# Value product in bursts over eight query blocks instead of four, with V fetched per head group from DRAM

## The chip, the cores and the metric

The kernel runs on one core of one Trainium2 chip. The metric is device time in microseconds (us), from the runs of the program before the change: 726.66, 725.91 and 726.65 us, median 726.65 us. One further execution was taken with the hardware profiler; it lasted 726.8 us.

## What is computed

Two branches of one block are mixed by a learned gate. Branch A is attention over 2048 positions with 32 heads of 16 columns and a sliding causal window of 256; branch B is a gated linear unit.

```python
qkv = x @ wqkv                                    # x: 2048 x 512
scores = einsum("bhqd,bhkd->bhqk", q, k) * 16 ** -0.5
mask = (i - j >= 0) & (i - j < 256)               # i: query, j: key
p = softmax(where(mask, scores, -1e9))
a = einsum("bhqk,bhkd->bhqd", p, v) @ wo
b = (sigmoid(x_ @ w_gate) * (x_ @ w_up)) @ w_down # x_ is the same x
g = sigmoid((x * gate_w).sum(-1))
return g * a + (1 - g) * b
```

All of it is fp32. The kernel takes one x for both branches.

## The kernel before

**Tiles and stages.** The 2048 positions are 16 blocks of 128. The 32 heads are 8 head groups of 4. So attention has 128 steps, called blocks here and `u` in the code; `u // 16` is the head group. The first 40 us project V and the first queries and keys. Then the loop over `u` runs from 0 to 137 (lines 796 to 919), and the last stage (lines 969 to 1032) multiplies by `w_down` and `wo` and writes the output.

**What a block does.** For each of the 4 heads, called a slot here, TensorE computes the scores of query block `u` (`s_part`, line 334, tile `s`). VectorE adds the mask and takes each row's maximum (line 350, tile `junk`); this is called the reduction below. Nine blocks later TensorE computes the transposed scores of key block `u - 9` (`st_part`, line 385, tile `st`), with the maxima already inside through an extra row of the operands, and ScalarE takes the exponential into the tile `pbuf` (line 397). When all four heads of a block are there, GpSimd clears what lies outside the window with one or two `affine_select` (`mask_p`, lines 403 and 409). `s` and `st` have two PSUM banks each: the scores of a slot wait for the reduction of two slots before, the transposed scores for the exponential of two slots before.

**Side work on TensorE.** The `s` and `st` matmuls use half of the array's rows (64). In the other time both halves work through the gate and up projections (`gu`), the projections of later head groups (`pj`) and a tail (`tp`). One step of this is a turn: one 64x512 matmul on each half. `GAPS` (line 44) says how many turns follow each slot: twelve times 3, three times 2; the sixteenth slot of four blocks has none. Each such group is accumulated over 24 matmuls in one of three `misc` banks; a ScalarE copy (line 523 or 269) empties it before the group three further on may start.

**The value product.** Every four blocks, from `u = 13` on, there is a visit: `pv_part` (line 418) multiplies a strip of four query blocks by V. The four heads stand side by side in columns of 32 (`tile_position`), all 128 rows are used, in plain fp32:

```python
for j in range(j0, q0 + 4):
    q, e = max(j, q0), min(j + 3, q0 + 4)
    for hh in range(HG):
        v = j * VROW + (g * HG + hh) * VW
        mm(pv[32 * hh:32 * hh + 32, ...], Vf[:, v:v + 32], p_blk(...), ...)
```

It is written into the one bank `pv` and copied out by ScalarE (`o_take`, line 435) into the tile `ob`. Its last column of ones gives the softmax sums.

**The maxima.** At the same visits `max_split` (line 357) takes the sixteen maxima of a strip through three small VectorE instructions (lines 360, 361, 365), `max_store` sends them to DRAM and `max_load` brings them back as rows of the operand ring. The strip is the one whose transposed scores begin two blocks later.

**What sets the order.** The order on TensorE, ScalarE, VectorE and the SP queue, which issues the DMAs, is written out by this loop. Side work of VectorE (low parts of split operands, list `behind`) is taken at slots 1, 5 and 9 after a visit, that of ScalarE (list `acts`) at any slot but the last three. V lies in SBUF for all heads (tile `V`, block after block); `pbuf` holds 15 block places.

Of the kernel before, what the change touches and what calls it, by code (L numbers as in the profile page):

```python
# [14 lines left out]
P = 128  # L15
# [3 lines left out]
H = 32  # L19
# [13 lines left out]
VROW = H * VW  # L33
SCALE = DH ** -0.5
# [5 lines left out]
PVLAG = LAG + 4  # L40
SD = 3
QB = 32
HOLD = 3
GAPS = [3] * 12 + [2] * 3
SHIFT = 6
# [9 lines left out]
AHEAD = 7  # L55
H_LOAD = {126: (0,), 130: (1, 2), 134: (3, 4), 137: (5, 6)}
# [3 lines left out]
def gated_mix_kernel(  # L60
# [37 lines left out]
    stack_d = nc.dram_tensor("stack_scratch", (RING, 2, P, CH2), F32, kind="Internal").ap()  # L98
    fill_d = nc.dram_tensor("fill_scratch", (2, CH2), F32, kind="Internal").ap()
# [39 lines left out]
    with ExitStack() as actx:  # L139
# [4 lines left out]

        Vf = apool.tile([P, NB * VROW + 16], F32, name="V")
        Vh = Vf[:, 0:NB * VROW].rearrange("p (b h w) -> p b h w", b=NB, w=VW)
# [22 lines left out]
        xraw = Vf[:, NB * VROW + 16 - 2 * ND * CH:].rearrange("p (c d t) -> p c d t", c=2, d=ND)  # L169
# [57 lines left out]
        def fill_v(b0, b1):  # L227
            if b1 == NB:
                nc.gpsimd.memset(Vf[:, NB * VROW:], 0.0)
            nc.gpsimd.memset(Vh[:, b0:b1, :, DH:VW], 1.0)  # L230

        fill_v(0, NB // 2)

# [5 lines left out]
        def v_part(b, d):  # L239
# [4 lines left out]
            if d == ND - 1:  # L244
                nc.scalar.copy(Vh[:, b, :, 0:DH], vp.pop(b).rearrange("p (h w) -> p h w", w=DH))
# [21 lines left out]
        def proj_raw(s):  # L267
            raws[s] = cpool.tile([P, CH], F32, tag="sp", name=f"pr{s}", bufs=4)
            nc.scalar.copy(raws[s], pj[s])
            pj[s] = raws.pop(s)  # L270
# [86 lines left out]
        def max_split(s):  # L357
# [6 lines left out]
            nms[s] = spool.tile([P, QB], F32, tag="nt", name=f"nt{s}")  # L364
# [15 lines left out]

        def p_blk(u, hh, a, n):
            s0, step = homes[u // 4 % 2][u % 4]
            return pbuf[:, s0 + a * step:s0 + (a + n - 1) * step + 1:step, hh]
# [17 lines left out]
        def mask_p(u):  # L401
            s0, step = homes[u // 4 % 2][u % 4]
            nc.gpsimd.affine_select(  # L403
                pbuf[:, s0], pbuf[:, s0], pattern=[[0, HG], [1, P]], compare_op=ALU.is_ge,
                fill=0.0, base=0, channel_multiplier=-1,
            )
            if u % NB + 2 < NB:
                old = pbuf[:, s0 + 2 * step]
# [9 lines left out]
        def pv_part(s):  # L418
# [3 lines left out]
            for j in range(j0, q0 + 4):  # L422
                q, e = max(j, q0), min(j + 3, q0 + 4)
                for hh in range(HG):
                    v = j * VROW + (g * HG + hh) * VW
                    mm(  # L426
                        pv[32 * hh:32 * hh + 32, (q - q0) * P:(e - q0) * P],
                        Vf[:, v:v + 32],
# [4 lines left out]
            evac.append(lambda: o_take(s))  # L433

        def o_take(s):
            g, c = divmod(s, NC)
            ob = cpool.tile([P, CH], F32, tag="ob", name=f"ob{s}", bufs=1)
            nc.scalar.copy(ob, pv)
# [28 lines left out]
        def v_out(b):  # L467
            nc.scalar.copy(Vh[:, b, :, 0:DH], vq[b].rearrange("p (h w) -> p h w", w=DH))
# [52 lines left out]
        def gu_post(f, c, w):  # L521
            t = cpool.tile([P, CH], F32, tag="sp", name=f"sp{f}_{c}_{w}", bufs=4)
# [42 lines left out]
        def tail_post(b):  # L565
            t = cpool.tile([P, CH], F32, tag="sp", name=f"tt{b}", bufs=4)
# [34 lines left out]
        def v_sum(b):  # L601
            lower, upper = halves.pop(f"vh{b}")
            t = cpool.tile([P, CH], F32, tag="sp", name=f"vsum{b}", bufs=4)
            nc.scalar.copy(t, lower)
            heads = lambda v: v.rearrange("p (h w) -> p h w", w=DH)
            behind.append(lambda: nc.vector.tensor_tensor(Vh[:, b, :, 0:DH], heads(upper), heads(t), op=ALU.add))
# [8 lines left out]
        def proj_sum(s):  # L615
            lower, upper = halves.pop(f"ph{s}")
            t = cpool.tile([P, CH], F32, tag="sp", name=f"psum{s}", bufs=4)
# [37 lines left out]
        def turns():  # L655
# [3 lines left out]
            sizes = GAPS * ((NU - PVLAG + 4) // 4) + GAPS[0:12]  # L659
            sizes += [6] * 14  # L660
            for size in sizes:
                for _ in range(size):
# [4 lines left out]
                    for half, v in enumerate((t, t - SHIFT)):  # L667
                        if 0 <= v < n_rest * k3:
# [3 lines left out]
                            if k == 0 and n in ended and size > 3:  # L672
# [118 lines left out]

        proj_at = {5: [5], LAG: [6, 7], U_LAST: [NSTEP - 2], U_LAST + 1: [NSTEP - 1]}
# [291 lines left out]
```

## Time and profile before

| what | value |
|---|---|
| median of the runs | 726.65 us |
| profiled execution, and the span of its trace | 726.8 us, 725.1 us |
| TensorE busy in the span (matmul, weight load) | 719.6 us, 590.4 us |
| VectorE, ScalarE, GpSimd busy | 485.0, 422.4, 163.5 us |
| value product matmuls (line 426) | 1408 records, 32 visits, from 83.1 to 553.3 us |
| reductions (line 350) | 512, mean 0.53 us |
| clock granted to TensorE | full speed in every slice |

A matmul's row gives its start and a modelled end, and matmuls overlap, so TensorE reads as busy nearly all the time whether or not its array is filled. What a piece costs is therefore read from the distance between the starts of the matmuls around it. An fp32 matmul leaves two records (passes): a visit of 24 matmuls has 48.

### The profile page before, as it was taken

Reading aid. Unit: us, or ns where it says so; the run is one execution under the profiler, and the core shown is the slowest. Engines: PE = TensorE matmul, PEld = TensorE weight load, DVE = VectorE, ACT = ScalarE, POOL = GpSimd, SP = SyncE. Lnnn points to the kernel's source line nnn. Section 1 sums busy time; section 2 is a strip of 40 time slices with the busy share of each in tenths; the row PEclk is TensorE's granted clock in tenths of the full one; section 3 lists DMA queues with packets and bytes.
Section 4 is the critical chain, followed back from the end, with each engine's and each line's share of the span. In section 5 each row is a group of like instructions: output and inputs, shape, how many; then the busy total and the mean of one; then the engine's idle time right before and its main releaser. Section 6 shows DMA issues by size and latency. Waiting matters only on the chain.

```text
span 725.1 us, 17392 instructions
## 1 busy us (share of the span) xinstructions
PE 719.6 (99%) x6298; PEld 590.4 (81%) x6298; DVE 485.0 (67%) x1455; ACT 422.4 (58%) x890; POOL 163.5 (23%) x255
## 2 busy tenths in 40 slices
PE   9999999999999999999999999999999999999997
PEld 7888888888888788887888877888788888888886
DVE  5368767666775676767677676677837777667481
ACT  6423766666576576756667666665666654535341
POOL 5200333232233223323223332322431000000000
PEclk9999999999999999999999999999999999999999
DMA  8442335444454543454444355354478897878431
GB/s 291 123 117 80 126 128 209 158 151 132 148 189 151 190 132 132 157 184 166 154 148 162 116 197 184 131 187 141 132 226 209 220 256 192 227 173 245 141 67 58
DMA packets 99502, 118.30 MB, mean 163 GB/s; under 512 B 46526, under 2 KB 59326, under 8 KB 99416
## 3 DMA queue, kind: packets, MB, share of 16 engines
q1 hardware_dynamic: 99272, 117.07, 52.2%
q8 instruction: 49, 0.80, 0.5%
q14 instruction: 37, 0.30, 0.1%
q10 hardware_dynamic: 144, 0.13, 0.1%
HBM read 67.34 MB, written 46.67 MB: 157 GB/s over the span
## 4 chain that ended last, share of the span: by engine, by line
PE 98%; DMA 1%; SPq 0%; issue 0%; ACT 0%; DVE 0%; DVEq 0%
PE gu L257 28%; PE pj L257 12%; PE pv L426 11%; PE s L344 7%; PE st L392 6%; PE tp L561 6%; PE pd L89 5%; PE pd L88 5%; PE pd L90 5%; PE vh L598 3%; PE pa L88 2%; PE pa L90 2%; PE pa L89 2%; PE vps L464 1%; DMA V<-in_xT_dram 1%; PE pd L1011 1%
## 5 line engine op out<-in xcount | busy, mean ns | idle before, releaser
L350 DVE CUSTOM_DVE_ANT_0 junk<-s,mask 128x384 f32<-128x384 f32 (+2 forms) x512 | 272.1, 531 | 138.8 <-PE s L344 69.8
L397 ACT ACTIVATE pbuf<-st 128x384 f32<-128x384 f32 (+2 forms) x512 | 240.9, 477 | 161.9 <-PE st L392 105.9
L257 PE MATMUL gu<-xh,w 64*128 64x512 f32 x1152 | 271.0, 393 | 0.0
L257 PE MATMUL gu<-xl,w 64*128 64x512 f32 x576 | 182.5, 391 | 0.0
L403 POOL TENSOR_SCALAR_AFFINE_SELECT pbuf<-pbuf 128x512 f32<-128x512 f32 x128 | 82.7, 646 | 368.7 <-ACT pbuf L397 368.7
L392 PE MATMUL st<-ring 64*128 64x384 f32 (+2 forms) x536 | 165.7, 326 | 0.0
L344 PE MATMUL s<-ring 64*128 64x384 f32 (+2 forms) x536 | 163.3, 323 | 0.0
L257 PEld LDWEIGHTS gu<-xh,w 64*128 64x128 f32 x1152 | 150.4, 185 | 12.4
L344 PEld LDWEIGHTS s<-ring 64*128 64x128 f32 x536 | 95.2, 184 | 16.3 <-issue 4.5
L392 PEld LDWEIGHTS st<-ring 64*128 64x128 f32 x536 | 95.8, 184 | 7.3 <-PE pv L426 0.4
L257 PEld LDWEIGHTS gu<-xl,w 64*128 64x128 f32 x576 | 87.7, 185 | 4.2
L426 PE MATMUL pv<-pbuf,V 128*32 128x384 f32 (+2 forms) x1408 | 84.3, 386 | 0.0
L257 PE MATMUL pj<-xh,wqh 64*128 64x512 f32 (+1 forms) x228 | 80.5, 394 | 0.0
L257 PE MATMUL pj<-xl,wqh 64*128 64x512 f32 (+1 forms) x228 | 80.2, 393 | 0.0
L426 PEld LDWEIGHTS pv<-pbuf,V 128*32 128x32 f32 x1408 | 41.5, 110 | 40.6 <-issue 30.2
L409 POOL TENSOR_SCALAR_AFFINE_SELECT pbuf<-pbuf 128x512 f32<-128x512 f32 x112 | 71.5, 639 | 0.0
L257 PE MATMUL pj<-xh,wql 64*128 64x512 f32 (+1 forms) x228 | 70.4, 393 | 0.0
L88 PE MATMUL pd<-ring,hb 128*128 128x512 f32 x160 | 62.3, 389 | 0.0
L90 PE MATMUL pd<-ring,hb 128*128 128x512 f32 x160 | 62.3, 389 | 0.0
L89 PE MATMUL pd<-ring,hb 128*128 128x512 f32 x160 | 62.2, 389 | 0.0
L84 ACT CAST hb<-V 128x512 fp32r<-128x512 f32 x40 | 24.9, 622 | 56.7 <-DVE V L762 46.9
L257 PEld LDWEIGHTS pj<-xh,wql 64*128 64x128 f32 (+1 forms) x228 | 41.0, 185 | 2.8
(127 smaller groups left out, 1104.7 us busy)
## 6 DMA issues: line engine op xcount, KB each, us to landing
gu_scratch<-sp SPq DMA_DIRECT2D x72, 256.0 KB
V<-gu_scratch SPq DMA_DIRECT2D x36, 512.0 KB
ring<-stack_scratch SPq DMA_DIRECT2D x56, 256.0 KB
stack_scratch<-sh SPq DMA_DIRECT2D x14, 512.0 KB
stack_scratch<-sl SPq DMA_DIRECT2D x14, 512.0 KB
ring<-stack_scratch SPq DMA_DIRECT2D x14, 512.0 KB
guraw<-in_wgu_dram SPq DMA_DIRECT2D x18, 256.0 KB
oT_scratch<-ob SPq DMA_DIRECT2D x128, 32.0 KB
```

The lines of the kernel that those rows point to most:

```text
L88: mm(ps, lh, rh, start=first, stop=False)
L89: mm(ps, lh, rl, start=False, stop=False)
L90: mm(ps, ll, rh, start=False, stop=last)
L257: return mm(pt, (wl if w == 2 else wh)[r, d], (xl if w == 1 else xh)[r, d, c * CH:(c + 1) * CH], start=k == 0 and not second, stop=k == 3 ...
L344: mm(pt[:, (k - k0) * P:(e - k0) * P], lhsT, blk(g, k, hh, 1, e - k), start=k == k0, stop=e == i + 1, skip_group_check=True,)
L350: nc.vector.tensor_tensor_reduce(junk[:, 0:n], pt[:, 0:n], mask[:, 3 * P - n:], scale=1.0, scalar=NEG, op0=ALU.add, op1=ALU.max, accum_out ...
L392: mm(pt[:, (q - j) * P:(e - j) * P], lhsT, blk(g, q, hh, 0, e - q), start=q == j, stop=e == last, skip_group_check=True,)
L397: exps.append(nc.scalar.activation(p_blk(u, hh, 0, n), pt[:, 0:n * P].rearrange("p (b t) -> p b t", t=P), AF.Exp, scale=SCALE,))
L403: nc.gpsimd.affine_select(pbuf[:, s0], pbuf[:, s0], pattern=[[0, HG], [1, P]], compare_op=ALU.is_ge, fill=0.0, base=0, channel_multiplier=-1,)
L409: nc.gpsimd.affine_select(old, old, pattern=[[0, HG], [-1, P]], compare_op=ALU.is_gt, fill=0.0, base=0, channel_multiplier=1,)
L426: mm(pv[32 * hh:32 * hh + 32, (q - q0) * P:(e - q0) * P], Vf[:, v:v + 32], p_blk(g * NB + j, hh, q - j, e - q), start=j == j0, stop=j == q ...
L561: return mm(tp[b][:, 0:TW], (xl if w == 1 else xh)[r, d, b * P:(b + 1) * P], tw[d][int(w == 2)][r, 0:TW], start=k == 0 and not second, sto ...
```

## The change

The value product of the first seven head groups is done in fourteen double visits, at `u = 17, 25, ... 121`. Each takes two strips of four query blocks, one after the other. The second strip is accumulated in a bank borrowed from the transposed scores (tag `st`). The last head group keeps its four single visits. The maxima keep their rhythm of four blocks (`mark`), so every second `max_split` now stands in a stretch without a value product.

Twice as many exponentials must be kept. They go into the SBUF place of V (`pwide`, 15 block places), and V, laid out by head group, is stored to DRAM in four pieces (at `u = 2, 3, 6, 10`) and read back one head group at a time (`vt`, 0.56 MB, at `u = 12, 28, ... 108` and 122).

The turns of eight blocks, 84 as before, are spread over 31 slots instead of 30: the slots numbered 3, 7, 11, 15, 19, 23 and 28 to 30 have two turns, the others three, and the thirty-second none. VectorE's side work is taken at slots 1, 5, 9, 13, 18, 22, 26 of the 32, with up to four pieces and two of ScalarE put into the double visit itself. `ob` moves into the pool `sp` (5 buffers instead of 4); the split maxima have one buffer instead of two. In the turns, a group's second half now always waits for an exponential that was issued after its first half ended.

```diff
+WIDE = 2 * 4
+NWIDE = NG - 1
+GAPS2 = [2 if i % 4 == 3 and i < 24 or i > 27 else 3 for i in range(31)]
+V_STORE = {2: 0, 3: 1, 6: 2, 10: 3}
+V_LOAD = {122: 7, **{16 * g + 12: g for g in range(7)}}
...
+        vt = Vf[:, VT:VT + NB * HG * VW]
+        pwide = Vf[:, 0:VT].rearrange("p (s h t) -> p s h t", h=HG, t=P)
+
+        def v_store(q):
+            n = 4 * HG * VW
+            nc.sync.dma_start(
+                v_d.rearrange("g p (q x) -> q p g x", q=4)[q],
+                Vf[:, q * NG * n:(q + 1) * NG * n].rearrange("p (g x) -> p g x", g=NG),
+            )
+
+        def v_load(g):
+            nc.sync.dma_start(vt, v_d[g])
...
+        def p_home(u):
+            if u // NB >= NWIDE:
+                return pbuf, *homes[u // 4 % 2][u % 4]
+            if u % WIDE < 4:
+                return pbuf, u % 4 * 3, 1
+            return pwide, *homes[u // WIDE % 2][u % 4]
...
-        def pv_part(s):
+        def pv_part(s, bank):
...
-                    v = j * VROW + (g * HG + hh) * VW
+                    v = (j * HG + hh) * VW
+                    w = min(32, NB * HG * VW - v)
                     mm(
-                        pv[32 * hh:32 * hh + 32, (q - q0) * P:(e - q0) * P],
-                        Vf[:, v:v + 32],
+                        bank[32 * hh:32 * hh + w, (q - q0) * P:(e - q0) * P],
+                        vt[:, v:v + w],
...
-        def o_take(s):
+        def o_take(s, bank):
             g, c = divmod(s, NC)
-            ob = cpool.tile([P, CH], F32, tag="ob", name=f"ob{s}", bufs=1)
-            nc.scalar.copy(ob, pv)
+            ob = cpool.tile([P, CH], F32, tag="sp", name=f"ob{s}", bufs=5)
+            nc.scalar.copy(ob, bank)
...
-            sizes = GAPS * ((NU - PVLAG + 4) // 4) + GAPS[0:12]
+            sizes = GAPS2 * (NB * NWIDE // WIDE) + GAPS + GAPS[0:12]
...
-                            if k == 0 and n in ended and size > 3:
+                            if k == 0 and n in ended:
                                 after(ins, exps[ended[n]])
...
+        U_WIDE = NB * NWIDE + LAG
+        visits = {u: 2 for u in range(PVLAG + 4, U_WIDE + 1, WIDE)}
+        visits.update({u: 1 for u in range(U_WIDE + 4, N, 4)})
...
-                if hh == 0 and u >= PVLAG and (u - PVLAG) % 4 == 0:
-                    pv_part((u - PVLAG) // 4)
-                    if visit:
-                        max_split((u - 5) // 4)
-                        run_dmas(later)
-                        later.clear()
-                        max_store((u - 5) // 4)
-                if hh == 2 and visit:
+                wide = visits.get(u) == 2
+                if hh == 0 and u in visits:
+                    s2 = (u - PVLAG) // 4 - wide
+                    pv_part(s2, pv)
+                if hh == 0 and mark:
+                    max_split((u - 5) // 4)
+                    run_dmas(later)
+                    later.clear()
+                    max_store((u - 5) // 4)
+                if hh == 0 and wide:
+                    flush(evac)
+                    o_take(s2, pv)
+                    run_dmas(later)
+                    later.clear()
+                    max_load((u - 5) // 4)
+                    second = ps.tile([P, CH], F32, tag="st", name=f"pv{s2}", bufs=2)
+                    pv_part(s2 + 1, second)
+                    for guests, n in ((acts, 2), (behind, 4)):
+                        for _ in range(min(n, len(guests))):
+                            guests.pop(0)()
+                    o_take(s2 + 1, second)
+                elif hh == 0 and u in visits:
+                    evac.append(lambda s2=s2: o_take(s2, pv))
+                if hh == 2 and mark:
                     transfers()
```

**The order at three places.** Numbers behind a name tell tiles apart; `s45_0` is the score tile of block 45, head 0. The first place is TensorE at block 45. Before, the last slot of block 44 has no turns and a visit follows:

```order
L344 MATMUL s44_3_3227<-ring_63 128x384
L392 MATMUL st35_2_3231<-ring_63 128x384
L426 MATMUL pv_868<-pbuf_867,V_73 32x384 x8
L426 MATMUL pv_868<-pbuf_867,V_73 32x256 x4
L426 MATMUL pv_868<-pbuf_867,V_73 32x128 x4
L344 MATMUL s45_0_3258<-ring_63 128x384
L392 MATMUL st36_1_3262<-ring_63 128x384
```

Now the same slot has two turns, and block 45 begins straight behind them:

```order
L368 MATMUL s44_3_3240<-ring_63 128x384
L423 MATMUL st35_2_3244<-ring_63 128x384
L281 MATMUL gu2_2_1_3220<-xh_70,w0_72 128x512
L281 MATMUL gu2_0_1_3143<-xh_70,w0_72 128x512
L281 MATMUL gu2_2_1_3220<-xl_71,w0_72 128x512
L281 MATMUL gu2_0_1_3143<-xl_71,w0_72 128x512
L368 MATMUL s45_0_3259<-ring_63 128x384
L423 MATMUL st36_1_3263<-ring_63 128x384
```

Before block 41, where a single visit stood, TensorE now has both strips in a row (`pv_870` is the bank `pv`, `pv6_2984` the borrowed one, `V_73` as an operand of the last ones both `vt` and `pwide`):

```order
L423 MATMUL st31_2_2940<-ring_63 128x128
L458 MATMUL pv_870<-V_73 32x128 x4
L458 MATMUL pv_870<-V_73 32x256 x4
L458 MATMUL pv_870<-pbuf_869,V_73 32x384 x8
L458 MATMUL pv_870<-pbuf_869,V_73 32x256 x4
L458 MATMUL pv_870<-pbuf_869,V_73 32x128 x4
L458 MATMUL pv6_2984<-pbuf_869,V_73 32x128 x4
L458 MATMUL pv6_2984<-pbuf_869,V_73 32x256 x4
L458 MATMUL pv6_2984<-V_73 32x384 x8
L458 MATMUL pv6_2984<-V_73 32x256 x4
L458 MATMUL pv6_2984<-V_73 32x128 x3
L458 MATMUL pv6_2984<-V_73 17x128
```

The visit of block 45 has moved into that of block 49. The second place is VectorE at block 45, where the order itself barely changes: the three instructions of `max_split` (`nm10`, `nt10`) stood between the reductions of blocks 44 and 45 before:

```order
L350 ISA junk44_3_3229,mx11_3191<-s44_3_3227,mask_154 128x384
L350 ISA mx11_3191 128x1
L360 TENSOR_SCALAR nm10_3252<-mx10_2921 128x4x4
L361 SCALAR_TENSOR_TENSOR nm10_3252<-mx10_2921,nm10_3252 128x4x4
L365 STREAM_TRANSPOSE nt10_3255<-nm10_3252 128x32
L350 ISA junk45_0_3260,mx11_3191<-s45_0_3258,mask_154 128x384
```

and stand there now, with a low part (`sl14`, slot 18) two reductions further on:

```order
L374 ISA junk44_3_3242,mx11_3196<-s44_3_3240,mask_154 128x384
L374 ISA mx11_3196 128x1
L384 TENSOR_SCALAR nm10_3253<-mx10_2899 128x4x4
L385 SCALAR_TENSOR_TENSOR nm10_3253<-mx10_2899,nm10_3253 128x4x4
L389 STREAM_TRANSPOSE nt10_3256<-nm10_3253 128x32
L374 ISA junk45_0_3261,mx11_3196<-s45_0_3259,mask_154 128x384
L374 ISA mx11_3196 128x1
L374 ISA junk45_1_3274,mx11_3196<-s45_1_3272,mask_154 128x384
L374 ISA mx11_3196 128x1
L374 ISA junk45_2_3289,mx11_3196<-s45_2_3287,mask_154 128x384
L374 ISA mx11_3196 128x1
L308 TENSOR_TENSOR sl14_3170<-pr15_3154,sh14_3169 128x512
```

What moved is the visit around it: TensorE was in its value product there, and now goes on with scores. Such a low part stands at slot 18 in 11 of the 14 marks without a visit, and at slot 13, three slots ahead of the mark, in 10 of them. The third place is TensorE between blocks 26 and 27. Before, the group `gu1_2_0` ends in slot `s26_1`, and `gu1_3_0`, which takes over its bank, starts three slots later, as the first matmul behind `s27_0`:

```order
L344 MATMUL s26_3_2044<-ring_63 128x384
L392 MATMUL st17_2_2048<-ring_63 128x384
L257 MATMUL pj10_2008<-xh_70,wql2_996 128x512
L257 MATMUL pj11_2038<-xl_71,wqh2_995 128x512
L257 MATMUL pj10_2008<-xh_70,wql2_996 128x512
L257 MATMUL pj11_2038<-xh_70,wqh2_995 128x512
L257 MATMUL pj10_2008<-xh_70,wql2_996 128x512
L257 MATMUL pj11_2038<-xl_71,wqh2_995 128x512
L344 MATMUL s27_0_2061<-ring_63 128x384
L392 MATMUL st18_1_2065<-ring_63 128x384
L257 MATMUL gu1_3_0_2071<-xh_70,w0_72 128x512
```

Now `gu1_2_0` ends in the first turn of slot `s26_2`, its copy follows the exponential of `s26_3`'s slot, and `gu1_3_0` starts in the third turn behind `s27_0`, two slots later, with a slot of two turns between:

```order
L423 MATMUL st17_2_2050<-ring_63 128x384
L281 MATMUL pj10_2012<-xh_70,wql2_995 128x512
L281 MATMUL pj11_2042<-xh_70,wqh2_994 128x512
L281 MATMUL pj10_2012<-xh_70,wql2_995 128x512
L281 MATMUL pj11_2042<-xl_71,wqh2_994 128x512
L368 MATMUL s27_0_2063<-ring_63 128x384
L423 MATMUL st18_1_2067<-ring_63 128x384
L281 MATMUL pj10_2012<-xh_70,wql2_995 128x512
L281 MATMUL pj11_2042<-xl_71,wqh2_994 128x512
L281 MATMUL pj10_2012<-xh_70,wql2_995 128x512
L281 MATMUL pj11_2042<-xl_71,wqh2_994 128x512
L281 MATMUL gu1_3_0_2077<-xh_70,w0_72 128x512
```

Nine hand-overs of a bank stand like this one now; eight more leave two slots with other turns between; before, all in this stretch leave three slots.

66 lines of the change are left out of this document (38 added, 28 removed).

## The prediction

> **What bounds the kernel now.** First the page's busy times, its chain and its DMA totals:
>
> ```profile
> PE 719.6 (99%) x6298; PEld 590.4 (81%) x6298; DVE 485.0 (67%) x1455; ACT 422.4 (58%) x890; POOL 163.5 (23%) x255
> DMA packets 99502, 118.30 MB, mean 163 GB/s; under 512 B 46526, under 2 KB 59326, under 8 KB 99416
> PE 98%; DMA 1%; SPq 0%; issue 0%; ACT 0%; DVE 0%; DVEq 0%
> ```
>
> TensorE alone sets the time. The change takes no matmul away, so it can only gain from gaps between matmuls, and lose by making TensorE wait. Both are read from starts. The timeline of TensorE around the visit at 296 us (columns: start, duration, engine, line):
>
> ```profile
> 294.18 0.33 PE L344 MATMUL s<-ring 64*128 64x384 f32 x1
> ...
> 296.11 0.33 PE L344 MATMUL s<-ring 64*128 64x384 f32 x1
> 296.39 2.80 PE L426 MATMUL pv<-pbuf,V 128*32 128x128 f32 x48
> 299.12 0.44 PE L344 MATMUL s<-ring 64*128 64x384 f32 x1
> ...
> 300.10 0.33 PE L344 MATMUL s<-ring 64*128 64x384 f32 x1
> ...
> 302.70 0.34 PE L344 MATMUL s<-ring 64*128 64x384 f32 x1
> ...
> 303.34 0.40 PE L257 MATMUL gu<-xh,w 64*128 64x512 f32 x2
> ```
>
> A score matmul opens each slot. A slot of three turns costs (302.70 - 300.10) / 3 = 0.867 us, one of two turns (296.11 - 294.18) / 3 = 0.643, so a turn costs 0.224 and a slot without turns should cost 0.195. Around the visit it is more: the last slot costs 296.39 - 296.11 = 0.28 (0.09 extra), the first one 300.10 - 299.12 = 0.98 (0.11 extra). The visit itself takes 2.73. In the chain of waits in order of time, a head group's first strip and a later one:
>
> ```profile
> 266.28 2.08 PE pv L426 x32
> ...
> 311.73 2.73 PE pv L426 x48
> ...
> 327.31 2.08 PE pv L426 x32
> ```
>
> A first strip has 9 blocks of 128 columns, a later one 12, so a block costs 0.65 / 3 = 0.217 and a visit has 2.73 - 12 x 0.217 = 0.13 of its own. Together a visit costs 0.09 + 0.11 + 0.13 = 0.33 us beside its work.
>
> [...]
>
> A second reading: from 266.28 to 327.31, 61.03 us, stand 48 slots of three turns (41.62), 12 of two (7.72), 4 without (0.78) and 45 strip blocks (9.77), together 59.89. The rest is 1.14, and 0.78 more because a sixteenth of the score columns is missing at a group's ends (64 x 0.195 / 16): 1.92 over four visits, 0.48 each.
>
> **What the change saves.** Fourteen visits vanish into their neighbours. At 0.33 to 0.48 each that is 4.6 to 6.7 us; I take 0.39, nearer to the row-by-row reading: **5.5 us**. Turns (84 in eight blocks) and slots (32) stay the same, so nothing else is saved.
>
> **What it adds: VectorE at the marks without a visit.** The split of the maxima lies inside a visit today, where the next reduction waits for TensorE anyway. At fourteen marks that cover is gone. A reduction, a low part and the distance of reductions, in VectorE's timeline after that visit:
>
> ```profile
> 300.47 0.56 DVE L350 CUSTOM_DVE_ANT_0 junk<-s,mask 128x384 f32<-128x384 f32 x1 [0.30 <-PE s L344]
> 300.95 0.08 DVE L350 DVE_READ_ACCUMULATOR2_ANT mx<- 128x1 f32 x1
> 300.95 0.69 DVE L284 TENSOR_TENSOR sl<-pr,sh 128x512 fp32r<-128x512 f32 x1
> 301.56 0.55 DVE L350 CUSTOM_DVE_ANT_0 junk<-s,mask 128x384 f32<-128x384 f32 x1
> ...
> 302.26 0.56 DVE L350 CUSTOM_DVE_ANT_0 junk<-s,mask 128x384 f32<-128x384 f32 x1
> ```
>
> A reduction starts 0.37 us after its slot (300.47 to 300.10), the next can follow 0.70 later (301.56 to 302.26), and a low part between makes that 1.09. A slot may start when the reduction of two slots before is done, 0.56 to 0.70 after that one's start. So a reduction may be 2 x 0.867 - 0.37 - 0.56 (or 0.70) = 0.66 to 0.80 late before TensorE waits, and VectorE recovers 0.867 - 0.70 = 0.17 a slot. The split, in the same engine's timeline at 297 us with GpSimd's masks beside it, and at 342 us without:
>
> ```profile
> 297.16 0.56 DVE L360 TENSOR_SCALAR nm<-mx 128x16 fp32r<-128x16 f32 x1
> 297.76 0.55 DVE L361 SCALAR_TENSOR_TENSOR nm<-mx,nm 128x16 fp32r<-128x16 f32 x1
> 298.35 0.21 DVE L365 STREAM_TRANSPOSE nt<-nm 128x32 f32<-128x32 f32 x1
> ```
>
> ```profile
> 297.06 0.63 POOL L403 TENSOR_SCALAR_AFFINE_SELECT pbuf<-pbuf 128x512 f32<-128x512 f32 x1 [1.54 <-ACT pbuf L397]
> 297.65 0.63 POOL L409 TENSOR_SCALAR_AFFINE_SELECT pbuf<-pbuf 128x512 f32<-128x512 f32 x1
> ```
>
> ```profile
> 342.39 0.17 DVE L360 TENSOR_SCALAR nm<-mx 128x16 fp32r<-128x16 f32 x1
> 342.60 0.17 DVE L361 SCALAR_TENSOR_TENSOR nm<-mx,nm 128x16 fp32r<-128x16 f32 x1
> 342.81 0.21 DVE L365 STREAM_TRANSPOSE nt<-nm 128x32 f32<-128x32 f32 x1
> ```
>
> Free, the split takes 0.63 us. Beside masks each of its first two instructions ends just after a mask does (297.72 after 297.69, 298.31 after 298.28), and it takes 1.40. At a mark, the slot ahead has two turns. Its reduction starts at +0.37, the split at +0.85 (0.48 later, as 300.95 after 300.47), which is 0.21 after the mark's slot begins. The first mask starts 0.96 after the slot ahead (297.06 to 296.10), 0.32 after the mark's slot. So the split's first instruction just gets through, the second (at 0.42) is caught by the first mask until about 0.98, and the next reduction starts at about 1.23, 0.86 late. TensorE then waits 0.06 to 0.20; I take 0.13 x 14 = **1.8 us**. In 11 of these marks a low part follows two slots on (0.39 more, with 0.3 recovered and a shorter two-turn slot next): 0 to 0.15, I take 0.07 x 11 = **0.8 us**.
>
> **What it adds: banks handed over sooner.** ScalarE's timeline has the copies:
>
> ```profile
> 300.08 0.58 ACT L438 COPY ob<-pv 128x512 f32<-128x512 f32 x1
> ...
> 303.16 0.49 ACT L397 ACTIVATE pbuf<-st 128x384 f32<-128x384 f32 x1 [0.44 <-PE st L392]
> 303.55 0.58 ACT L523 COPY sp<-gu 128x512 f32<-128x512 f32 x1
> ```
>
> A copy that follows the exponential of its slot ends at 304.13, 1.43 after the slot's start (302.70). In nine places the next group then wants the bank in the third turn of the next slot, with a two-turn slot between: 0.643 + (303.34 - 302.70) = 1.28 after that start. TensorE waits 0.15 x 9 = 1.35; eight more places come out within 0.1 of nothing, 0.2 in all. Together **1.5 us**; 0 if the copies end 0.15 sooner, 3 if a copy in the slot before delays the exponential by 0.1. Before, three slots left 0.4 or more.
>
> **What I cost at nothing.** The new wait of a group's second half: its exponential ends at 303.65, 0.95 after its slot, and the waiting turn comes 1.28 after it or later, so 0.3 covers it. The borrowed bank: its copy (0.58) stands first on ScalarE behind a double visit, and the slot that needs the bank begins 0.98 after the first; if the copy starts 0.4 late, it costs up to 0.1 a visit, 1.4 in all. V from DRAM: a load of 0.56 MB takes 3.4 us at the mean 163 GB/s and is issued five blocks (19 us, at 61.03 / 16 a block) ahead; without that cover the first strip of a group would wait. On SP it stands ahead of a mark's `max_store`, four slots early. The four stores of V (1.1 MB, 6.8 us each at that rate) are in the queue ahead of the first maxima; the last is issued three blocks (11 us) before the first exponential goes into V's place, and if it took longer, ScalarE would wait once, 1 or 2 us. The strips' copies share five `sp` buffers with the side work; a copy that found none free would hold up the exponentials behind it, and nothing in this trace shows one that does. The maxima's trip through DRAM, from the SP queue's timeline:
>
> ```profile
> 53.69 0.33 SPq L368 DMA_DIRECT2D max_scratch<-nt  x1
> 55.15 1.27 SPq L375 DMA_DIRECT2D ring<-max_scratch  x2
> ```
>
> Store to load takes 1.46 us. With the split done at 1.2, a second load 0.6 later and as long a landing again, the rows are there 4.8 after the mark, and wanted eight slots on, at 6 x 0.867 + 2 x 0.643 = 6.5. The cover is 1.7.
>
> **The sum.** Against the profiled execution: 726.8 - 5.5 + 1.8 + 0.8 + 1.5 = 725.4. It stood 0.15 above the median of the runs, so the forecast is **725.2 us**. About 0.2% (1.45 us) is what a measurement of this kernel can tell from no change, so this lies on that edge.
>
> **The rivals.**
> *The waits don't appear.* A reduction that frees its bank after 0.56, a copy that begins at its exponential's end, and a split that gets through ahead of the mask (it is short by 0.1 to 0.2 us everywhere) would leave only the saving: 726.65 - 5.5 = 721.2, up to 723. For it: today's slots show no such wait at all. Against it: all three margins are computed from undisturbed slots.
> *Slower: the split is caught whole.* In 10 of the 14 marks a low part stands three slots ahead of the split and leaves VectorE 0.05 late, so the split starts 0.26 after the mark's slot, the mask 0.32: the point is 0.06 us. If it is later, it ends 1.50 after the mask's start (297.06 to 298.56), the next reduction starts at 1.82, 1.45 late, and TensorE waits 0.65 to 0.79, 0.72 in the middle, with 0.18 more at the low part behind: 0.9 x 10 + 0.13 x 4 = 9.5. 726.65 - 5.5 + 1.5 + 9.5 = 732.1. For it: at 297 us it is caught so. Against it: there VectorE was behind from three slots of two turns.
> [...]
> [...]
> *V or the maxima late.* If queues eat the 1.7 us, 1 us at seven marks: 732 at most, more likely 727.
>
> **How the numbers follow.** The forecast has 0.45 (its own range 723.5 to 727: 0.22 faster, 0.20 same, 0.03 slower), no waits 0.25 (faster), the caught split 0.18 (slower), strips that don't join 0.05 (same), late transfers 0.07 (0.02 same, 0.05 slower). Faster 0.47, same 0.27, slower 0.26. The range 721.2 to 731.0 leaves out a part of the caught split and little else.
>
> **What would show it.** Right: eight blocks of score slots with no 0.28 and 0.98 slots in the middle, double visits of about 5.3 us; at the slot two behind a mark and at third turns such as behind `s27_0`, waits of 0.1 to 0.2 us for VectorE and ScalarE. Wrong: a pause between the strips; no waits; waits of 0.6 us or more at the marks; TensorE waiting for a DMA.

## The result, and the profile after

The changed kernel takes 739.3 us (median of 4 runs, 738.06 to 739.59); the kernel before, on the same chip, 726.58 (725.91 to 726.66). The ratio is 1.0174, with a 95% interval of 1.0156 to 1.0192: **slower by 12.7 us**. The forecast was 725.2, with a range from 721.2 to 731.0. The profiled execution took 739.34 us, with a span of 737.5.

The page of the changed kernel, its busy times, DMA totals and chain:

```profile
PE 728.0 (99%) x6298; PEld 592.0 (80%) x6298; DVE 479.3 (65%) x1455; ACT 427.4 (58%) x890; POOL 163.0 (22%) x254
DMA packets 104814, 127.22 MB, mean 173 GB/s; under 512 B 46718, under 2 KB 63614, under 8 KB 104728
PE 98%; DMA 1%; issue 0%; DVE 0%; DVEq 0%; SPq 0%
```

TensorE has the same 6298 matmul records and is still busy 99% of the span. But its busy time grew from 719.6 to 728.0 us, 8.4 of the 12.4 us by which the span grew (725.1 to 737.5), so a share of 99% hides the loss. The chain has 1% of DMA, as before. By lines, though, it was the first load of x before (`DMA V<-in_xT_dram 1%`), and now it is the maxima's store and load (`DMA max_scratch<-nt 1%; DMA ring<-max_scratch 1%`): the first sign of where to look. TensorE's timeline around the double visit at 249 us (start, duration, engine, line):

```profile
248.77 0.35 PE L368 MATMUL s<-ring 64*128 64x384 f32 x1
249.05 0.86 PE L458 MATMUL pv<-V 128*32 128x128 f32 x16
249.72 2.77 PE L458 MATMUL pv<-pbuf,V 128*32 128x384 f32 x48
252.31 2.12 PE L458 MATMUL pv<-V 128*32 128x384 f32 x32
254.36 0.44 PE L368 MATMUL s<-ring 64*128 64x384 f32 x1
255.33 0.33 PE L368 MATMUL s<-ring 64*128 64x384 f32 x1
```

The burst itself is what the change meant. The last slot takes 0.28 us, the double visit 254.36 - 249.05 = 5.31, the first slot 0.97, and nothing stands between the strips. The other double visits look the same (5.3 us, and 4.67 for the seven that hold a group's shorter first strip). So the loss is elsewhere. The table of waits, for the kernel before (one line) and for the changed one (what waited, for whom, us in total, times, longest):

```profile
PEld s L344 <- DVE mx L350: 1.0, 3, 0.3
```

```profile
PEld s L368 <- DVE mx L374: 8.4, 27, 0.5
PEld st L423 <- issue: 4.6, 1, 4.6
PE st L423 <- DMA ring<-max_scratch: 4.5, 2, 4.2
PEld gu L281 <- ACT sp L554: 3.6, 12, 0.4
PEld gu L281 <- ACT pr L293: 2.3, 7, 0.4
PEld pj L281 <- ACT sp L554: 0.7, 4, 0.2
```

Three kinds of wait are new or larger: score matmuls for VectorE at the marks (before, 1.6 us more stood under the split's `nm`, now 0.2), side matmuls for ScalarE's copies of their banks, and once, for over 4 us, a transposed-score matmul for the maxima from DRAM. The second and third row are one idle stretch, seen from the weight load and from the matmul. This is the place, on TensorE, two blocks behind the mark of block 109:

```profile
459.41 0.33 PE L368 MATMUL s<-ring 64*128 64x384 f32 x1
463.99 0.41 PE L423 MATMUL st<-ring 64*128 64x384 f32 x1 [4.25 <-DMA ring<-max_scratch]
```

and this is SP's queue ahead of it, where the maxima's store (L392) and load (L399) stand among other transfers:

```profile
450.11 0.34 SPq L342 DMA_DIRECT2D gu_scratch<-sp  x1
450.55 0.38 SPq L165 DMA_DIRECT2D V<-v_scratch  x1
450.98 1.55 SPq L531 DMA_DIRECT2D guraw<-in_wgu_dram  x1
452.58 0.42 SPq L571 DMA_DIRECT2D tailraw<-in_wgu_tail_dram  x1
453.05 0.43 SPq L342 DMA_DIRECT2D stack_scratch<-sh  x1
453.58 0.38 SPq L342 DMA_DIRECT2D stack_scratch<-sl  x1
454.05 2.22 SPq L342 DMA_DIRECT2D gu_scratch<-sp  x2
456.36 1.05 SPq L392 DMA_DIRECT2D max_scratch<-nt  x1
461.89 1.20 SPq L399 DMA_DIRECT2D ring<-max_scratch  x2
```

The mark began at 452.60. VectorE's split ended 1.3 us later, as forecast. But the store left 3.8 us behind the mark, because four stores of `later` are issued ahead of it and SP was busy with them until 456.27. It landed 5.5 us later, not 1.46, with 2.8 MB issued just ahead of it (256 KB for each of three gu stores and for guraw, 544 of V, 225 of the tail, twice 512 of the stack). SP waited 4.4 of the 5.5 us for this landing. What the landing itself waited for no view shows. That it was the transfers ahead is the author's estimate, from 5.5 us here, where the DMA engines were 98% busy from 452 to 459 us, and 1.46 at 53.69 us, where they were 7% busy until the load.

A second loss follows. The windows around the idle stretch (busy us of each engine and its instructions, granted clock, DMA share, GB/s):

```profile
452.00:459.00 7.00, 7.00 (x66) 5.66 (x64) 6.07 (x22) 4.71 (x10) 2.44 (x4) 1.00 0.98 350
459.00:464.00 5.00, 0.76 (x9) 0.37 (x5) 1.13 (x4) 0.49 (x1) 1.22 (x2) 1.00 0.18 61
464.00:471.00 7.00, 7.00 (x51) 6.92 (x51) 3.13 (x13) 4.88 (x11) 1.22 (x2) 0.76 0.33 111
465.00:468.00 3.00, 3.00 (x18) 3.00 (x17) 1.56 (x5) 2.08 (x5) 0.00 (x0) 0.50 0.28 105
```

The DMA engines were 98% busy before, and in the 7 us after the idle stretch TensorE was granted 0.76 of its clock. That is a mean: the last row shows half the clock, and a mean of 0.76 over 7 us is half the clock for 7 x 0.24 / 0.5 = 3.4 us, a loss of 1.7 us. Between the double visits that begin at 434.16 and 471.26 stand 471.26 - 434.16 - 5.32 = 31.78 us, in the twelve other such rows 25.2 to 27.1. This row alone lost 6 us: 4.25 of idle time and 1.7 by the clock.

Last, a loss where nothing was changed. The last stage's matmuls, before and after (count, busy us, mean ns):

```profile
L88 PE MATMUL pd<-ring,hb 128*128 128x512 f32 x160 | 62.3, 389 | 0.0
```

```profile
L94 PE MATMUL pd<-ring,hb 128*128 128x512 f32 x160 | 63.3, 396 | 0.0
```

There are 512 of them (three lines of 160 and two of 16), 7 ns longer each, and by their starts in the trace they follow each other 6 or 7 ns later than before (233 in place of 227 in the mean): 3 us in all. The change touches none of them. It made the tile `V` 192 bytes longer and took one 128-byte buffer of `nt` away, so `hb`, which lies behind both, starts 64 bytes further on.

### The profile page after: what moved, and what is told of

Same layout as the page of the kernel before. It is cut to its first block, busy times and chain, and to the rows that moved or that the text cites. A ratio compares the mean times of both kernels' runs of the same rounds, so it can differ in the third digit from the quotient of the medians.

```text
span 737.5 us, 17524 instructions
## 1 busy us (share of the span) xinstructions
PE 728.0 (99%) x6298; PEld 592.0 (80%) x6298; DVE 479.3 (65%) x1455; ACT 427.4 (58%) x890; POOL 163.0 (22%) x254
## 4 chain that ended last, share of the span: by engine, by line
PE 98%; DMA 1%; issue 0%; DVE 0%; DVEq 0%; SPq 0%
PE gu L281 28%; PE pj L281 12%; PE pv L458 11%; PE s L368 6%; PE tp L592 6%; PE st L423 5%; PE pd L94 5%; PE pd L96 5%; PE pd L95 5%; PE vh L629 3%; PE pa L94 2%; PE pa L96 2%; PE pa L95 2%; PE vps L495 2%; DMA max_scratch<-nt 1%; DMA ring<-max_scratch 1%
## 5 line engine op out<-in xcount | busy, mean ns | idle before, releaser
L281 PE MATMUL gu<-xl,w 64*128 64x512 f32 x576 | 185.1, 393 | 0.0
L428 ACT ACTIVATE pbuf<-st 128x384 f32<-128x384 f32 (+2 forms) x288 | 139.7, 491 | 60.1 <-PE st L423 30.8
L281 PEld LDWEIGHTS gu<-xh,w 64*128 64x128 f32 x1152 | 153.4, 185 | 15.1 <-ACT sp L554 3.6
L428 ACT ACTIVATE V<-st 128x384 f32<-128x384 f32 (+2 forms) x224 | 101.5, 455 | 54.2 <-PE st L423 27.7
L434 POOL TENSOR_SCALAR_AFFINE_SELECT pbuf<-pbuf 128x512 f32<-128x512 f32 x72 | 46.7, 649 | 260.1 <-ACT pbuf L428 203.2
L281 PEld LDWEIGHTS gu<-xl,w 64*128 64x128 f32 x576 | 89.8, 186 | 5.1
L94 PE MATMUL pd<-ring,hb 128*128 128x512 f32 x160 | 63.3, 396 | 0.0
L95 PE MATMUL pd<-ring,hb 128*128 128x512 f32 x160 | 63.3, 396 | 0.0
L96 PE MATMUL pd<-ring,hb 128*128 128x512 f32 x160 | 63.3, 395 | 0.0
L434 POOL TENSOR_SCALAR_AFFINE_SELECT V<-V 128x512 f32<-128x512 f32 x56 | 35.5, 635 | 119.0 <-ACT V L428 114.6
L469 ACT COPY ob<-pv 128x512 f32<-128x512 f32 x32 | 18.8, 586 | 54.5 <-PE pv L458 53.5
L458 PE MATMUL pv<-pbuf,V 128*32 128x384 f32 (+2 forms) x848 | 49.5, 381 | 0.0
```

The lines of the kernel that those rows point to most:

```text
L94: mm(ps, lh, rh, start=first, stop=False)
L95: mm(ps, lh, rl, start=False, stop=False)
L96: mm(ps, ll, rh, start=False, stop=last)
L281: return mm(pt, (wl if w == 2 else wh)[r, d], (xl if w == 1 else xh)[r, d, c * CH:(c + 1) * CH], start=k == 0 and not second, stop=k == 3 ...
L428: exps.append(nc.scalar.activation(p_blk(u, hh, 0, n), pt[:, 0:n * P].rearrange("p (b t) -> p b t", t=P), AF.Exp, scale=SCALE,))
L434: nc.gpsimd.affine_select(buf[:, s0], buf[:, s0], pattern=[[0, HG], [1, P]], compare_op=ALU.is_ge, fill=0.0, base=0, channel_multiplier=-1,)
```

## The experiments

Theories after the result: **A**, the place of `hb` makes the last stage longer; **B**, the maxima are late because of what stands ahead of them in SP's queue; **C**, banks are handed over too soon for ScalarE's copies; **D**, the uncovered split on VectorE. The rival to A, B and C in each case is that something else, such as the traffic of V or the work of ScalarE as a whole, is behind it.

**`align`.** The gate's sigmoid is written in place, so everything behind one 64-byte tile moves down and `hb` starts at a multiple of 128 bytes again:

```
-    gs = cpool.tile([P, NB], F32, name="gs")
-        nc.scalar.activation(gs, gsum, AF.Sigmoid)
+        nc.scalar.activation(gsum, gsum, AF.Sigmoid)
...
```

> The changed kernel with one 64-byte tile less (the gate's sigmoid is written in place), so that every tile behind it starts 64 bytes lower and the last stage's tile hb starts at a multiple of 128 bytes, as it did before the change; ring starts at such a multiple in all kernels. Theory A, place: the last stage's pd matmuls took 396 ns in the changed kernel and 389 before because hb and ring stand in different halves of a 128-byte line; they go back to 389 ns, and the time from 739.3 to about 736.3 us, all of it behind 546 us. Rival, something of the work beside (transfers, clock, a busier ScalarE): they stay at 396 ns, and the time at 739.3.

Measured: 735.93 us, ratio to before 1.0128 (1.0113 to 1.0143), 3.4 us less than the changed kernel. The row of the last stage:

```profile
L95 PE MATMUL pd<-ring,hb 128*128 128x512 f32 x160 | 62.3, 389 | 0.0
```

**`before_shift`**, the opposite edit, on the kernel before:

```
-        Vf = apool.tile([P, NB * VROW + 16], F32, name="V")
+        Vf = apool.tile([P, NB * VROW + 32], F32, name="V")
...
```

> The kernel before with V's tile 64 bytes longer and nothing else changed, so that hb starts 64 bytes behind a multiple of 128, as in the changed kernel. Theory A, place: pd matmuls go from 389 to 396 ns, the last stage (from 537 us on) is 3 us longer, 726.6 becomes about 729.6; the few pj matmuls over all 128 rows, whose weights come to stand like xh, go from 395 to 389 ns. Rival: no change, 726.6.

Measured: 729.17 us, ratio 1.0038 (1.0024 to 1.0052), 2.8 us more than before:

```profile
L88 PE MATMUL pd<-ring,hb 128*128 128x512 f32 x160 | 63.4, 396 | 0.0
```

Theory A holds in both directions. One part missed: the pj matmuls over all rows stayed at 394 to 397 ns, though modulo 128 bytes their weights now stood like `xh`. In the changed kernel, where they were not edited either, they take 389:

```profile
L281 PE MATMUL pj<-xh,wqh 128*128 128x512 f32 x20 | 7.8, 389 | 0.0
```

The sizes of the tiles explain both, if 256 bytes count and not 128. Between the start of `xh` and that of pj's weights lie `xl`, `w0`, `V` and `mask`. They are 110144 bytes before, which is 64 over a multiple of 256; 110208 in `before_shift`, 128 over; and 110336 in the changed kernel, an exact multiple.

**`before_both`** and **`before_shift32`** ask what about the place counts. The first puts a 64-byte tile ahead of `ring`, so that `ring` and `hb` shift together; the second makes `V` 32 bytes longer, so that `hb` alone shifts by 32.

```
+    front = cpool.tile([P, 16], F32, name="front")
     ring_t = cpool.tile([P, 4, RING * CH2], F32R, name="ring")
...
```

> The kernel before with a tile of 64 bytes ahead of ring, so that ring and hb both start 64 bytes behind a multiple of 128 (the run with hb alone shifted had pd at 396 ns and 729.2 us in all). Theory A in its first form, the two operands' places against each other count: both in the same half, pd at 389 ns, 726.5 us. Rival, hb's own place against a multiple of 128 bytes counts: 396 ns, 729.2 us.

> The kernel before with V's tile 32 bytes longer, so that hb starts 32 bytes behind a multiple of 128 and of 64. If only the half of a 128-byte line counts, hb's weights start in the first half, like ring, and pd stays at 389 ns, 726.5 us; if any start off a multiple of 64 or 128 costs: 396 ns or more, 729 us or more.

Measured: 726.62 us, ratio 1.0000 (0.9991 to 1.0010), with pd at 389 ns; and 730.39, ratio 1.0056 (1.0041 to 1.0071), with 396:

```profile
L88 PE MATMUL pd<-ring,hb 128*128 128x512 f32 x160 | 62.3, 389 | 0.0
```

```profile
L88 PE MATMUL pd<-ring,hb 128*128 128x512 f32 x160 | 63.3, 396 | 0.0
```

So it is the place of the two operands against each other, not that of `hb` alone. A difference of 32 or of 64 bytes costs these matmuls the same 6 to 7 ns. In the kernel before, `hb` starts 208640 bytes behind `ring`, a multiple of 256, so pd agrees with pj: 389 ns at a difference of 0 modulo 256 and 394 to 397 at 32 or 64, as pj took 389 at 0 and 394 to 397 at 64, 96 or 128.

**`v_early`** moves V's load away from the mark:

```
-V_LOAD = {122: 7, **{16 * g + 12: g for g in range(7)}}
+V_LOAD = {12: 0, 122: 7, **{16 * g + 10: g for g in range(1, 7)}}
```

> The changed kernel with V's load for groups 1 to 6 two blocks earlier (block 16g+10 in place of 16g+12), so that it no longer stands on SP just ahead of the maxima's store of the mark at 16g+13. Theory B, late maxima: at the mark of block 109 the store waited 5.5 us for its landing behind 2.6 MB of queued transfers, 0.56 MB of them V; without V the way is about 3 us shorter, the 4.6 us idle of the scores at 459 us goes nearly away, the granted clock of the following 7 us stays at 1.00 in place of 0.78, and the time falls by 5 to 6 us to about 733.5. Rival, the two 512 KB stack stores and the tail load are enough: an idle of 2 to 4 us stays, the time falls by 1 to 3 to 737. Rival, V's load has no part in it: 739.3.

Measured: 737.63 us, ratio 1.0152 (1.0137 to 1.0167), 1.7 less. The row before 469 us came down from 31.8 to 30.3, the idle stretch of the weight loads from 4.6 to 3.2. The clock still fell behind it, to a mean of 0.79 from 460 to 465 us and of 0.87 from 465 to 470, so 5 x (0.21 + 0.13) = 1.7 us stayed lost. Most of the gain came from SP: the store left 2.7 us behind the mark in place of 3.8, and store to load still took 459.69 - 454.43 = 5.26 us. V's load has a part in it, the smaller one; it was also still issued only 4.3 us ahead of the mark (2.1 before this edit).

**`store_first`** changes the order of SP's instructions at a mark:

```
                     max_split((u - 5) // 4)
+                    max_store((u - 5) // 4)
                     run_dmas(later)
                     later.clear()
-                    max_store((u - 5) // 4)
```

> The changed kernel with the maxima's store issued on SP ahead of the other stores at a mark (of the stack, gu, attention output), not behind them; V's load stays where it is. Theory B, queue of stores: at the mark of block 109 two 512 KB stack stores and two of gu stood between the split and the store, so the store leaves 2 to 3 us sooner and with 1.5 MB less ahead of it; the idle at 459 us (4.6 us) and the low clock behind it (0.78 for 7 us) go, row 459 to 471 gets as short as the others, 31.8 becomes 25.5 us, the time 739.3 becomes about 733. Rival, V and the loads issued before are what the maxima's way waits for: 2 us at most, 737 (moving V alone gave 1.7).

Measured: 733.63 us, ratio 1.0099 (1.0084 to 1.0114), 5.7 less. SP's queue at the same mark, and the windows behind it:

```profile
452.49 0.33 SPq L392 DMA_DIRECT2D max_scratch<-nt  x1
452.86 0.43 SPq L342 DMA_DIRECT2D stack_scratch<-sh  x1
453.34 0.43 SPq L342 DMA_DIRECT2D stack_scratch<-sl  x1
453.86 2.09 SPq L342 DMA_DIRECT2D gu_scratch<-sp  x2
456.06 1.64 SPq L399 DMA_DIRECT2D ring<-max_scratch  x2
```

```profile
455.00:460.00 5.00, 4.10 (x36) 3.19 (x34) 3.24 (x12) 2.32 (x5) 2.42 (x4) 1.00 0.90 321
460.00:465.00 5.00, 5.00 (x51) 4.75 (x51) 3.19 (x14) 4.52 (x11) 1.22 (x2) 1.00 0.29 107
```

Store to load is 3.6 us now, and part of that is SP issuing the other stores in between. The transposed scores wait 0.9 for the maxima in the table of waits, and the clock stays at 1.00. Theory B holds: it was the order on SP more than V.

**`gaps_even`** puts the nine short slots of a row into three runs:

```
-GAPS2 = [2 if i % 4 == 3 and i < 24 or i > 27 else 3 for i in range(31)]
+GAPS2 = [3] * 8 + [2] * 3 + [3] * 8 + [2] * 3 + [3] * 6 + [2] * 3
```

> The changed kernel with the nine slots of two turns in three runs of three (as before the change) in place of single ones spread over the row, so that all slots of three turns begin at a bank's third again. Theory C, banks: the waits of gu and pj matmuls for ScalarE's copies (3.6 and 2.3 us in the profile of the changed kernel, and 0.9 of pj) go, 0.3 us a cycle over 13.5 cycles, and the time falls by 4 us to about 735. Rival, the short slots cost it back because ScalarE and VectorE are the limit in a run of them: 739 or more.

Measured: 739.58 us, ratio 1.0180 (1.0164 to 1.0195): no difference. But its waits say why:

```profile
PEld s L368 <- DVE mx L374: 15.1, 44, 0.7
PEld gu L281 <- ACT sp L554: 0.6, 2, 0.3
```

The waits for copies went from 3.6 to 0.6 us (and the 2.3 for `pr` are gone), as theory C had it, and as much came back as waits for VectorE, 8.4 to 15.1, as the rival had it, though on VectorE alone. More than half of these 15.1 us (8.6) stand at two slots, in and right behind the run of short slots that follows the mark: a reduction every 0.70 us does not fit slots of 0.643, so VectorE, late by the split and a low part, cannot catch up there.

**`copy_first`** goes at the banks without touching the slots. ScalarE's copy of a finished bank is issued ahead of its slot's exponential:

```
+                took = bool(evac) and PVLAG < u < U_WIDE
+                if took:
+                    evac.pop(0)()
                 if u < NU:
                     s_part(u, hh)
...
```

> The changed kernel with ScalarE's copy that empties a finished bank issued ahead of the exponential of its slot, not behind it, in the rows of the seven head groups. Theory C, banks: the slots of 1.1 us (in place of 0.87) at the 9th and 21st of a row and the 1.09 + 0.41 + 1.35 us run ahead of them are TensorE waiting for that copy, 4.3 us over the 13 rows; they go, and the time falls from 739.3 to about 735. Rival, ScalarE's total work or another wait is what these slots show (as with the short slots in runs, which changed nothing): 738.5 to 740, the long slots stay or move.

Measured: 734.06 us, ratio 1.0109 (1.0093 to 1.0125), 5.2 less. A handover in the changed kernel, first on ScalarE, then on TensorE:

```profile
137.73 0.49 ACT L428 ACTIVATE pbuf<-st 128x384 f32<-128x384 f32 x1 [0.61 <-PE s L368]
138.11 0.58 ACT L554 COPY sp<-gu 128x512 f32<-128x512 f32 x1
```

```profile
138.37 0.38 PE L281 MATMUL pj<-xl,wqh 64*128 64x512 f32 x1
138.75 0.50 PE L281 MATMUL gu<-xh,w 64*128 64x512 f32 x1
```

The gu matmul starts at 138.75, just as the copy behind the exponential ends (138.11 + 0.58 = 138.69), where a turn (0.224) behind the matmul at 138.37 would be 138.59. With the copy first, no row of gu or pj waiting for `sp` or `pr` is left in the table. Theory C holds. The gain is even held back, because the waits for the maxima got longer when the rest was faster (4.6 and 1.9 us on PE and PEld in its table, in place of 4.5 and 0.6).

**`split_spread`** takes the split of the maxima at a mark without a visit apart, one operation in each of the three slots ahead of it (`max_split` takes the numbers of the operations that it issues):

```
+                if hh > 0 and PVLAG <= u + 1 < NU and (u + 1 - PVLAG) % 4 == 0 and visits.get(u + 1) != 2:
+                    max_split((u - 4) // 4, (hh - 1,))
...
```

> The changed kernel with VectorE's split of the maxima, at the marks without a visit, as one operation in each of the three slots ahead of the mark in place of three in a row at it; the maxima's store stays at the mark. Theory D, uncovered split: the slots at the mark (0.92, 0.98 and 0.96 us in place of 0.87 and less, about 0.25 us a mark) go back to 0.87, 13 marks, 3.3 us, and the time falls from 739.3 to about 736; the store leaves about 0.6 us earlier as well, which takes up to 0.6 us off the two late marks. Rival, these slots are long because of the reading of the maxima's rows or the low parts on VectorE: 739.3, the slots stay above 0.95.

Measured: 736.20 us, ratio 1.0135 (1.0120 to 1.0150), 3.1 less, and in the table of waits:

```profile
PEld s L368 <- DVE mx L374: 1.6, 5, 0.4
```

Theory D holds; 8.4 us of such waits were there, counted on the weight loads, of which 3.1 us came back as time.

**`all`** has the edits of `align`, `v_early`, `store_first`, `copy_first` and `split_spread` together.

> All of these together: 64 bytes lower tiles (3.4 us measured), V's load two blocks earlier and the maxima's store first (together 6 us of the late mark), the copy first (4.3), the split spread (3.3). If the four causes are what the change lost and add up: 739.3 - 3.4 - 6.3 - 0.6 - 4.3 - 3.3 = 721.4, 5 us below the kernel before. If the causes overlap (a wait taken away lets the next one show): 726 to 731, at best as the kernel before.

Measured: 725.25 us, ratio 0.9988 (0.9975 to 1.0001), not told apart from the kernel before. That is 14.1 us less than the changed kernel, and 4 short of the sum. What is left in its table:

```profile
PEld st L428 <- DMA ring<-max_scratch: 2.8, 2, 1.8
PE st L428 <- DMA ring<-max_scratch: 2.7, 3, 1.4
```

**`all_early`** lets the maxima leave earlier and V's load come behind the mark:

```
-V_LOAD = {12: 0, 122: 7, **{16 * g + 10: g for g in range(1, 7)}}
+V_LOAD = {12: 0, 122: 7, **{16 * g + 14: g for g in range(1, 7)}}
...
+                    if hh < 3:
+                        max_split((u - 4) // 4, (hh,))
+                    else:
+                        max_store((u - 4) // 4)
...
```

> The kernel with all four edits, but at the marks without a visit the split in the first three slots of the block ahead and the maxima's store in its fourth, about 1.7 us sooner, and V's load for groups 1 to 6 behind the mark (block 16g+14). In the kernel with all four edits three rows still waited for the maxima (26.4, 27.3 and 26.4 us in place of 25.0 to 25.3). Theory B, that what was left of the 4 us between the 721.4 expected there and the 725.25 measured is late maxima: these rows come down to 25.0 to 25.3 and the time to about 721.5. Rival, the causes overlap in another way: 724 to 726.

Measured: 722.61 us, ratio 0.9949 (0.9936 to 0.9963): **4.1 us faster than the kernel before**. One wait for the maxima is left:

```profile
PE st L428 <- DMA ring<-max_scratch: 0.3, 1, 0.3
```

The three rows that had waited come down from 26.4, 27.3 and 26.4 us to 25.5, 25.7 and 26.0, so a little is still lost there. The run moves the store and V's load at once; which of the two did more is not shown.

**`before_copy`** puts the copy first and the store first into the kernel before.

> The kernel before with those two of the edits that can be made to it: ScalarE's copy of a finished bank ahead of the exponential, and the maxima's store ahead of the other stores of a mark. It tells whether these edits gain by themselves or mend only what the change broke. If they mend: 726.4, within 0.5. If they are gains of their own: 722 to 724, and the bursts are then worth nothing like their 5.5 us.

Measured: 726.36 us, ratio 0.9998 (0.9989 to 1.0007). These two edits gain nothing by themselves; they mend what the change broke. The place of the tiles gains nothing there either, as pd already takes 389 ns. The split ahead of its mark was not tried on the kernel before, whose waits for VectorE were 1.0 + 1.6 us in all, so up to that much of the 4.1 us could be its own.

## Why the prediction was wrong

The saving was right in its form and nearly in its size. By the rows, two single visits with the slots around them cost 2 x (0.28 + 2.73 + 0.98) = 7.98 us; a double one costs 0.28 + 5.31 + 0.97 = 6.56, and the two slots that now stand elsewhere 0.195 + 0.867 = 1.06. That is 0.36 less a time, an estimate of 5.0 us for fourteen, where 5.5 was forecast. Once the losses are mended the kernel is 4.1 us faster than before. The runs that take one loss away each give the sizes of the rest:

| step of the prediction | forecast, us | measured, us |
|---|---|---|
| split and low part at the marks | 1.8 + 0.8 | 3.1 (`split_spread`) |
| banks handed over sooner | 1.5, 3 at most | 5.2 (`copy_first`) |
| the maxima's trip | 0 | 5.7 (`store_first`) |
| place of the tiles | not seen | 3.4 (`align`), 2.8 (`before_shift`) |

The four add up to 17.4 us, and `all_early`, which mends them together, is 16.7 below the changed kernel. With the estimated saving, 726.6 - 5.0 + 17.4 is 739.0, for 739.3 measured.

- **The step that failed most is "The maxima's trip through DRAM", costed at nothing with a cover of 1.7 us.** It took store to load, 1.46 us, from the mark at 53.69 us, the shortest of the 32 in the trace before; the others took 2.3 to 4.3. Most of those loads waited for other things too, but at 360 us SP was free from 362.74 on and waited for the landing:

```profile
359.81 0.33 SPq L368 DMA_DIRECT2D max_scratch<-nt  x1
363.21 1.19 SPq L375 DMA_DIRECT2D ring<-max_scratch  x2
```

  With these 3.40 us the way is 1.2 + 3.40 + 0.6 + 1.46 = 6.7, where the prediction had 4.8 (4.7 by its own terms), and 6.7 is past the 6.5 at which the rows are wanted. So the trace before already showed a landing too slow for the cover. The prediction also let the store leave when the split ends. At a mark the store stands on SP behind all that `later` holds and behind what was issued in the blocks ahead. The prediction even named that V's load "stands ahead of a mark's `max_store`", and did not price it. Where V, the stack's stores and the tail's load met, the way took 3.8 + 5.5 us to the load. The rival "V or the maxima late" named the right wait, with 1 us at seven marks. It was 6 us at one: 4.25 us idle, and behind it 3.4 us at half the clock, which no step of the prediction had.
- **The mis-sized term is the banks**, 5.2 us for 1.5. The mechanism is as described, down to the third turn of the next slot, but the prediction counted nine places with 0.15 us each; waits came at 24, up to 0.4 long (12 + 7 + 4 of them in the three rows quoted and one more of 0.2).
- **The step that was missing is the place of the tiles.** "Turns (84 in eight blocks) and slots (32) stay the same, so nothing else is saved" was taken to mean that nothing else is lost, and the sizes of tiles in the diff were not read as a change to stages behind them.
- **VectorE at the marks was right**, with 3.1 for 2.6. At all fourteen marks without a visit the split is caught just as described, its first instruction free (0.17 us) and its second beside a mask (0.52 to 0.62, and ending 24 to 27 ns behind that mask at each of the fourteen), and 13 of the 27 waits, 4.2 of the 8.4 us, stand at the slot two behind the mark. In VectorE's timeline at 267.7 us:

```profile
267.73 0.17 DVE L384 TENSOR_SCALAR nm<-mx 128x16 fp32r<-128x16 f32 x1
267.93 0.58 DVE L385 SCALAR_TENSOR_TENSOR nm<-mx,nm 128x16 fp32r<-128x16 f32 x1
268.54 0.21 DVE L389 STREAM_TRANSPOSE nt<-nm 128x32 f32<-128x32 f32 x1
```

  The rival that had it caught whole, with 9.5 us, did not happen. The prediction called that a matter of 0.06 us, so it was near.
- The second bank, the new wait of a group's second half and the shared `sp` buffers show no wait of their own in the table.

## What to carry to other kernels

A small transfer that something waits for is priced by what is issued ahead of it at that place, not by its own time somewhere quiet: the maxima's store took 1.46 us to the load at 53.69 us, and left 3.8 us late and took 5.5 at block 109. Issue it first; here that gave back 5.7 us (`store_first`). When tiles change size, compare the starts of the operands of every later matmul, not only of those that were edited: here 64 bytes cost 512 matmuls 6 to 7 ns each. A change that loses may hide a gain: the losses, taken away one at a time and then together, left this kernel 4.1 us faster than before.

## What the runs showed of the hardware

- Matmuls of 128x512 f32 over all rows (`pd` and `pj`) followed each other by 227 ns in the mean where the starts of their two operands in SBUF differed by a multiple of 256 bytes (`pd` before, `pj` in the changed kernel), and by 233 ns where they did not (`pj` before, `pd` in the changed kernel, both 64 over). The rows of all runs give 389 ns at 0 for both, and 394 to 397 ns at 32 and 64 for `pd` and at 64, 96 and 128 for `pj`, modulo 256. Why it is so is open.
- The granted clock fell to half, 0.50 from 465 to 468 us, behind an idle stretch of the matmuls of 4.25 us (the changed kernel). Its mean over the 7 us from 464 to 471 was 0.76 there, and 0.76 also in `gaps_even`, behind an idle stretch of 2.17 us; in `v_early`, behind 2.86 us, it was 0.79 and 0.87 in the two windows of 5 us from 460. Behind 1.39 us (`all`) it stayed at 1.00. That the idle stretch is the cause is the author's estimate from these four.
- The issue of one DMA on SP mostly took 0.3 to 0.6 us. Around the mark of block 109, where the DMA engines were 98% busy (452 to 459 us), it took 1.0 to 1.6 us for four of nine, and 0.3 to 0.4 for the others. So what stood behind such an issue on SP came up to 1.2 us later (1.55 against 0.34); what the issue waits for in that time the profile does not show.
